# Small first loads of q and k, first weights between two parts, and values used as loaded, in a fused attention and MLP kernel

## The chip, the cores and the metric

The kernel runs on one core of a Trainium2 chip. Times are device microseconds (us) of one execution; "span" is the profiled time from the first to the last instruction. The kernel before takes 306.58 us, the median of three runs (306.48 to 307.78). A difference counts as faster or slower from 2% on.

## The reference

Windowed attention (8 batches, 8 heads, 576 tokens, head size 64; each query sees keys at most 32 positions away), followed by an MLP over all 4608 tokens. Cut to what matters:

```python
scores = (1 / 8) * np.matmul(q, k.transpose(0, 1, 3, 2))
mask = np.abs(pos[:, None] - pos[None, :]) <= 32
attn = softmax(np.where(mask, scores, -1e9))          # without its rows' maximum in the kernel
x = np.matmul(attn, v)                                # -> (4608, 512)
h = x @ w_in                                          # (512, 2048)
out = (h * sigmoid(1.702 * h)) @ w_out                # (2048, 512)
```

## The kernel before

Tokens are worked on in units of 128. A unit is: transpose its keys and queries on TensorE, copy them out of PSUM (keys on VectorE, queries on ScalarE), scores, exp on ScalarE, multiply by a band mask on VectorE, multiply with the values, normalize on VectorE, transpose to xT. Two units make a tile, on which layer 1 (`h_ps`, then gelu) and layer 2 (`o_ps`) work. The program order is written by hand, and each engine runs its own queue in that order. Only the head, up to the first full layer-1 work, is touched by the change:

```python
# head(), order of issue; GpSimd's loads and VectorE's work are recorded in this order
self.load_first("k", 0); self.load_first("q", 0)     # heads 0,1 of 512 tokens, f32, on SyncE
self.setup()                                         # memsets, identity
for h in ((2, 4), (4, 8)):                           # the other heads, cast on the way
    for c in "kq": self.load_heads(0, c, h)
self.load_v(0); self.load_v(1); self.load_v(2, 0, 64)
self.setup_mask()                                    # GpSimd alone: memset, 4 selections
for c in "kq": self.load_edge(c)                     # tokens 512..575
self.load_w_in(0)                                    # first quarter of w_in
...
self.keep_busy(15)                                   # fillers: matmuls on zeros
self.pair_heads("k", 0, 0, dve, ...)                 # VectorE: cast of the first keys (kc)
self.pair_heads("q", 0, 0, act, ...)
...
self.values(0, "hh"); self.norm(0)
self.values(1, "ot"); self.norm(1)
self.x_T(0, "a", act)
self.edge_T("k", "a", dve); self.edge_T("q", "a", act)
self.band(2); self.x_T(1, "o", act); self.scores(3)
l1 = self.layer1_start()                             # first two pairs of layer 1, by halves
...
self.layer1(0, 2); self.x_T(2, "t")                  # second pair
self.layer1(0, 3); self.x_T(3, "o")
self.layer1(0, 4)                                    # from here on TensorE is full
```

A unit's odd half needs values that start 64 tokens later than they are loaded. `odd_v` makes them, by two copies a unit.

The softmax here doesn't subtract the row's maximum and nothing guards it: scores larger than these inputs give would overflow.

Of the kernel before, what the change touches and what calls it, by code (L numbers as in the profile page):

```python
# [27 lines left out]
class _Kernel:  # L28
# [7 lines left out]
    def __init__(self, ctx, tc, q, k, v, w_in, w_out, out):  # L36
        self.tc, self.nc = tc, tc.nc
        self.q, self.k, self.v, self.w_in, self.w_out, self.out = q, k, v, w_in, w_out, out
        self.B, self.H, self.S, self.D = q.shape
        self.N = self.B * self.S  # L40
        self.DM = self.H * self.D
        self.DFF = w_in.shape[1]
        self.NK = self.DM // 128
        self.NFF = self.DFF // 128
        self.scale = 1.0 / (self.D ** 0.5)
        self.NU = self.N // 128
        self.NW = self.NU // 2

        def pool(name, bufs, **kw):
            return ctx.enter_context(tc.tile_pool(name=name, bufs=bufs, **kw))  # L50

        self.cst = pool("cst", 1)
        self.work = pool("work", 2)
        self.ps = pool("ps", 1, space=bass.MemoryType.PSUM)
        self.stage, self.paired, self.turn = {}, set(), {}
        self.xT, self.g, self.o_ps = {}, {}, {}
        self.sc, self.p, self.acc, self.x, self.o_sb = {}, {}, {}, {}, []
# [10 lines left out]
    def setup(self):  # L68
        nc, cst = self.nc, self.cst
        self.ident = cst.tile([128, 128], BF16, name="ident")  # L70
        self.mask = cst.tile([128, 4, SQ], BF16, name="mask")
        self.w_in_sb = cst.tile([128, self.NK, self.DFF], BF16, name="w_in_sb")
# [13 lines left out]
        make_identity(nc, self.ident)  # L86
        for i in range(NV):
            nc.vector.memset(self.ve[i][:, :, self.D:], 1.0)  # L88

    def setup_mask(self):  # L90

        pool, m = self.nc.gpsimd, self.mask
        lo, hi = slice(0, 64), slice(64, 128)
        pool.memset(m, 1.0)
        for blks, rows, sign in ((slice(0, 2), lo, 1), (slice(0, 2), hi, -1), (slice(2, 4), lo, -1), (slice(2, 4), hi, 1)):
            ap = m[rows, blks, :].rearrange("p b (j s) -> p b j s", j=JT)
            pool.affine_select(out=ap, in_=ap, compare_op=ALU.is_ge, fill=0.0, base=0,  # L97
                               pattern=[[0, 2], [-sign, JT], [-sign * JT, SQ // JT]], channel_multiplier=sign)
# [28 lines left out]

    def load_heads(self, i, c, heads=None):

        key = (c, i)  # L130
        if key not in self.stage:
            self.stage[key] = self.work.tile([128, self.H, JT * self.D], BF16, name=c + "s", tag=c + "s", bufs=3)
        lo, hi = heads or (0, self.H)
        src = {"q": self.q, "k": self.k}[c]
        for off, b, s, m in self.pieces(512 * i, 512):
            self.nc.gpsimd.dma_start(self.stage[key][off // JT:(off + m) // JT, lo:hi, :],  # L136
                                     src[b, lo:hi, s:s + m, :].rearrange("h (p j) d -> p h (j d)", j=JT))
# [26 lines left out]
    def heads_T(self, c, i, hp, kind):  # L164


        tp = self.bank(kind, [128, JT, 128], BF16, "tp")
        for j in range(JT):
            if (c, i, hp) in self.paired:
                self.nc.tensor.transpose(tp[:, j, :], self.stage[c, i, "c"][:, hp, j], self.ident)  # L170
                continue
            for t in range(2):
                self.nc.tensor.transpose(tp[64 * t:64 * t + 64, j, :],
                                         self.stage[c, i][:, 2 * hp + t, j * self.D:(j + 1) * self.D], self.ident)
        return tp

    def keys_T(self, i, hp, kind="t", eng=None):
        tp = self.heads_T("k", i, hp, kind)
        at = (512 * i) % RING
        self.cast(eng or self.nc.vector, self.kT[:, hp, at:at + 512].rearrange("r (p j) -> r p j", j=JT),  # L180
                  tp.rearrange("r j p -> r p j"))

    def queries_T(self, i, hp, kind="t", eng=None):
        at = (128 * i) % RP
        tp = self.heads_T("q", i, hp, kind)
        self.cast(eng or nc.vector, self.qT[:, JT * hp:JT * hp + JT, at:at + 128], tp)

    def load_first(self, c, hp):

        raw = self.stage[c, "raw", hp] = self.cst.tile([128, 2, JT * self.D], F32, name=f"{c}_raw{hp}")  # L190
        src = {"q": self.q, "k": self.k}[c]
        self.nc.sync.dma_start(raw, src[0, 2 * hp:2 * hp + 2, 0:512, :].rearrange("h (p j) d -> p h (j d)", j=JT))

    def pair_heads(self, c, i, hp, eng, src=None):
# [3 lines left out]
        self.paired.add((c, i, hp))  # L198
        if src is None:
            src = self.stage[c, i][:, 2 * hp:2 * hp + 2, :]  # L200
        self.cast(eng, self.stage[c, i, "c"][:, hp], src.rearrange("p h (j d) -> p j h d", j=JT))
# [14 lines left out]

    def load_edge(self, c):

        self.stage[c, "edge"] = self.work.tile([64, self.H, self.D], BF16, name="edge", tag="edge")
        src = {"q": self.q, "k": self.k}[c]  # L220
        self.nc.gpsimd.dma_start(self.stage[c, "edge"], src[0, :, 512:576, :].rearrange("h s d -> s h d"))  # L221

    def edge_T(self, c, kind, eng):
        nc = self.nc
        src = self.stage[c, "edge"]
        tp = self.bank(kind, [128, 4, 64], BF16, "tp")
        for hp in range(4):
            nc.tensor.transpose(tp[:, hp, :], src[:, 2 * hp:2 * hp + 2, :], self.ident[:64, :64])
        if c == "k":
            self.cast(eng, self.kT[:, :, 512:576], tp)  # L230
        else:
            self.cast(eng, self.qT[:, :, 128:144].rearrange("r (h j) p -> r h j p", j=JT),
                      tp.rearrange("r h (p j) -> r h j p", j=JT))
# [24 lines left out]
    def band(self, u, hps=range(4)):  # L258
        p = self.p[u]
        cross = [(2 * u + i) % 9 == 8 for i in range(2)]  # L260
        a, b = 0 if cross[0] else 1, 2 if cross[1] else 3
        for eo in range(2):
            pv = p[:, eo, 2 * hps[0]:2 * hps[-1] + 2].rearrange("p (h b) s -> p h b s", b=2)
            msk = self.mask[:, a:b + 1:b - a, :].rearrange("p (o b) s -> p o b s", o=1)
            self.nc.vector.tensor_mul(pv, pv, msk.to_broadcast([128, len(hps), 2, SQ]))  # L265
# [54 lines left out]
    def values(self, u, kinds="aa"):  # L320
        nc, D = self.nc, self.D
        p = self.p.pop(u)
        acc = [self.bank(kinds[i], [128, 4, D + 1], F32, f"pv{i}") for i in range(2)]
        for half in range(2):
            for hh in range(4):
                h = 4 * half + hh
                for blk in range(2):
                    vt = (self.ve, self.vo)[blk][u % NV]
                    nc.tensor.matmul(acc[half][blk * 64:blk * 64 + 64, hh, :], p[:, h % 2, h // 2 * 2 + blk, :],  # L329
                                     vt[:, h, :D + 1], start=(hh == 0), stop=(hh == 3))  # L330
# [72 lines left out]
    def layer1_start(self):  # L403
# [3 lines left out]

        def unit(s):
            for d in range(2):
                self.products1(hps[d], 0, d, slice(128 * s, 128 * s + 128), s == 0, s == 1)  # L410
                if s:
                    self.nc.scalar.activation(g[:, 2 * d:2 * d + 2, :], hps[d], AF.Gelu_apprx_sigmoid)

        return unit
# [53 lines left out]
    def head(self):  # L468
# [5 lines left out]
        for h in ((2, 4), (4, 8)):  # L474
            for c in "kq":
                self.load_heads(0, c, h)
        for m in range(2):
            self.load_v(m)
        self.load_v(2, 0, 64)
        self.setup_mask()  # L480
        for c in "kq":
            self.load_edge(c)
        self.load_w_in(0)
# [17 lines left out]
        self.keep_busy(15)  # L501
        self.pair_heads("k", 0, 0, dve, self.stage["k", "raw", 0])
        self.pair_heads("q", 0, 0, act, self.stage["q", "raw", 0])
        for hp in range(2):
            self.keys_T(0, hp, "ht"[hp], dve)
            self.keep_busy(2)
            self.queries_T(0, hp, "ho"[hp], act)
            self.keep_busy(1 if hp else 2)
# [3 lines left out]
        self.keep_busy(5, "o")  # L512
        for hp in (2, 3):
            self.keys_T(0, hp, "ht"[hp % 2], dve)
        self.keep_busy(5, "o")
        for hp in (2, 3):
            self.queries_T(0, hp, "ho"[hp % 2], (act, dve)[hp % 2])
        self.keep_busy(1, "t")
        self.odd_v(0, dve)
        for u in range(2):  # L520
            self.scores(u, (2, 3))
        self.odd_v(1, act)
        self.band(0, (2, 3))
        self.keep_busy(5)
        self.scores(2)
        self.band(1, (2, 3))
# [4 lines left out]
        self.keep_busy(3)  # L531
        self.x_T(0, "a", act)
        self.edge_T("k", "a", dve)
        self.edge_T("q", "a", act)
        self.band(2)
        self.x_T(1, "o", act)
        self.scores(3)
        l1 = self.layer1_start()
        l1(0)
        self.band(3)  # L540
        self.odd_v(2, dve)
        self.odd_v(3, dve)
        l1(1)
# [24 lines left out]
        for hp in range(4):  # L568
            self.keys_T(1, hp, "a", dve)
            self.queries_T(1, hp, "a", act)  # L570
# [35 lines left out]
        for hp in range(4):  # L606
            self.keys_T(2, hp, "t", dve)
            if hp in (0, 1):
                self.pair_tile(2, (hp + 2,))
            self.queries_T(2, hp, "o", act)  # L610
# [22 lines left out]
    def window_4(self):  # L633
# [36 lines left out]
        for hp in range(4):  # L670
            self.queries_T(3, hp, "t", act)
# [116 lines left out]
```

## Time and profile before

| | kernel before |
|---|---|
| median | 306.58 us |
| span of the profiled run | 304.4 us |
| cast of the first keys | 3.71 us |
| second pair of layer 1 starts | 21.17 us |
| group of 96 layer-1 matmuls starts | 23.63 us |

On the page, these two lines tell that TensorE is the bound, and how much of the chain that ended last is not TensorE:

```profile
PE 291.9 (96%) x3395; PEld 203.8 (67%) x3429; DVE 132.5 (44%) x391; ACT 181.2 (60%) x310; POOL 128.6 (42%) x186
...
PE 89%; POOL 4%; DMA 3%; issue 1%; ACT 1%; DVE 0%; POOLq 0%
```

In the second line GpSimd (POOL) with its load issues and the landing of a weight load make up 7%, all of it in the head.

### The profile page before, as it was taken

To read this page: it belongs to the slowest core of one execution; us is meant where nothing else is said; L and a number is where in the kernel's file an instruction comes from. 1 tells how busy PE (TensorE), PEld (TensorE's weight loads), DVE (VectorE), ACT (ScalarE), POOL (GpSimd) and SP (SyncE) were. 2 spreads that over 40 slices of the span, in tenths; PEclk is the share of its full clock that TensorE was granted. 3 is DMA by queue.
4 is the path that set the end of the run, shared out by engine and by line. 5 is a ranking of instruction groups with operands and counts; after the bars stand their busy time and mean duration, and the time that the engine had idled before them with its cause. 6 is when DMAs were issued, how large, how long until landed. Compare 5 with 4: busy or idle time off the path is not lost.

```text
span 304.4 us, 8079 instructions
## 1 busy us (share of the span) xinstructions
PE 291.9 (96%) x3395; PEld 203.8 (67%) x3429; DVE 132.5 (44%) x391; ACT 181.2 (60%) x310; POOL 128.6 (42%) x186
## 2 busy tenths in 40 slices
PE   8789999999999999999999999999999999999992
PEld 5578755957666666666666666666666666666852
DVE  2681288675580807080708070807070708140011
ACT  3676464795866666666666666666666668424410
POOL 8963555696234363436343534343330301130120
PEclk9999999999999999999999999999999999999998
DMA  8999999999999999999999999999969626162112
GB/s 142 154 194 205 200 184 178 194 169 153 161 155 137 134 117 121 177 138 127 148 170 106 133 137 143 141 131 164 123 54 87 58 48 72 38 58 49 35 32 74
DMA packets 130325, 38.35 MB, mean 126 GB/s; under 512 B 111280, under 2 KB 128048, under 8 KB 130288
## 3 DMA queue, kind: packets, MB, share of 16 engines
q0 software_dynamic: 90032, 27.46, 94.8%
q1 hardware_dynamic: 40112, 10.30, 38.8%
q8 instruction: 27, 0.44, 0.7%
q14 instruction: 10, 0.08, 0.1%
q10 hardware_dynamic: 144, 0.07, 0.1%
HBM read 36.96 MB, written 9.44 MB: 152 GB/s over the span
## 4 chain that ended last, share of the span: by engine, by line
PE 89%; POOL 4%; DMA 3%; issue 1%; ACT 1%; DVE 0%; POOLq 0%
PE h_ps L399 40%; PE o_ps L423 40%; DMA w_in_sb<-in_moe_w_in_dram 3%; PE pv L347 3%; PE sc L285 2%; POOL ve L142 2%; PE tp L170 1%; PE o_ps L448 1%; PE sc L251 1%; PE pv L329 1%; POOL ks L136 1%; POOL qs L136 0%; POOL w_in_sb L112 0%; POOL mask L97 0%; POOL edge L221 0%
## 5 line engine op out<-in xcount | busy, mean ns | idle before, releaser
L399 PE MATMUL h_ps<-xT,w_in_sb 128*128 128x256 bf16 (+1 forms) x1168 | 130.6, 271 | 0.5 <-DMA w_in_sb<-in_moe_w_in_dram 0.3
L423 PE MATMUL o_ps<-w_out_sb,g 128*128 128x512 bf16 x526 | 125.3, 379 | 1.8 <-issue 0.2
L399 PEld LDWEIGHTS <-w_in_sb 128*128 128x128 bf16 x1168 | 112.3, 98 | 17.0 <-DMA w_in_sb<-in_moe_w_in_dram 0.9
L393 ACT ACTIVATE g<-h_ps 128x512 bf16<-128x512 f32 x142 | 84.7, 597 | 61.8 <-PE h_ps L399 61.7
L435 POOL DMA_DIRECT2D out_dram<-o_sb x70 | 44.2, 635 | 144.7 <-DVE rec L357 71.6
L423 PEld LDWEIGHTS <-g 128*128 128x128 bf16 x560 | 53.0, 98 | 57.8
L108 DVE COPY o_sb<-o_ps 128x512 f32<-128x512 f32 x34 | 23.4, 690 | 125.9 <-PE o_ps L423 125.9
L142 POOL DMA_DIRECT2D ve<-in_v_dram x41 | 35.5, 873 | 10.0 <-DMA w_out_sb<-in_moe_w_out_dram 2.8
L289 ACT ACTIVATE pp<-sc 128x512 bf16<-128x512 f32 x44 | 22.7, 602 | 24.7 <-PE sc L285 24.7
L149 POOL DMA_DIRECT2D kn<-in_k_dram x27 | 23.5, 876 | 4.5 <-DMA kn<-in_k_dram 1.9
L108 DVE COPY vo<-ve 64x528 bf16<-64x528 bf16 x69 | 22.5, 326 | 2.3 <-DMA ve<-in_v_dram 0.4
L358 DVE TENSOR_TENSOR x<-pv,rec 128x448 bf16<-128x448 f32 (+1 forms) x52 | 22.1, 425 | 1.8
L456 ACT ACT_TABLE_LOAD x13 | 16.7, 1283 | 0.2
L256 ACT ACTIVATE p<-sc 128x512 bf16<-128x512 f32 (+1 forms) x28 | 12.8, 541 | 2.7 <-PE sc L251 2.7
L108 ACT COPY qT<-tp 128x512 bf16<-128x512 bf16 (+1 forms) x16 | 9.1, 570 | 8.9 <-PE tp L170 6.1
L459 ACT ACT_TABLE_LOAD x11 | 14.1, 1283 | 0.2
L136 POOL DMA_DIRECT2D qs<-in_q_dram x17 | 12.1, 724 | 3.9 <-DMA w_out_sb<-in_moe_w_out_dram 1.8
L265 DVE TENSOR_TENSOR p<-p,mask 128x512 bf16<-128x512 bf16 (+1 forms) x28 | 9.8, 381 | 4.7 <-ACT p L256 2.3
L108 DVE COPY kT<-tp 128x512 bf16<-128x512 bf16 (+1 forms) x13 | 8.5, 658 | 5.1 <-PE tp L170 4.3
L347 PEld LDWEIGHTS <-pp 128*64 128x64 bf16 x384 | 7.1, 110 | 5.1 <-issue 5.1
L108 DVE COPY qc<-qs 128x512 bf16<-128x512 bf16 x32 | 9.3, 335 | 2.4 <-DMA qs<-in_q_dram 2.4
L465 PE MATMUL junk<-idle 128*128 128x256 bf16 x41 | 7.9, 333 | 1.5 <-DVE ve L88 1.1
(76 smaller groups left out, 179.2 us busy)
## 6 DMA issues: line engine op xcount, KB each, us to landing
out_dram<-o_sb POOLq DMA_DIRECT2D x70, 128.0 KB, 6.1
ve<-in_v_dram POOLq DMA_DIRECT2D x31, 128.0 KB, 8.5
kn<-in_k_dram POOLq DMA_DIRECT2D x21, 128.0 KB, 9.5
w_in_sb<-in_moe_w_in_dram POOLq DMA_DIRECT2D x4, 512.0 KB, 9.4
w_out_sb<-in_moe_w_out_dram POOLq DMA_DIRECT2D x4, 512.0 KB, 13.3
qs<-in_q_dram POOLq DMA_DIRECT2D x2, 448.0 KB, 13.2
qs<-in_q_dram POOLq DMA_DIRECT2D x3, 256.0 KB, 7.0
qs<-in_q_dram POOLq DMA_DIRECT2D x2, 384.0 KB, 10.5
```

The costliest lines, as they stand in the source:

```text
L108: (eng.copy if eng is self.nc.scalar else eng.tensor_copy)(out, in_)
L136: self.nc.gpsimd.dma_start(self.stage[key][off // JT:(off + m) // JT, lo:hi, :], src[b, lo:hi, s:s + m, :].rearrange("h (p j) d -> p h (j ...
L142: self.nc.gpsimd.dma_start(self.ve[m % NV][at:at + n, :, :self.D], self.v[b, :, s:s + n, :].rearrange("h s d -> s h d"))
L149: self.nc.gpsimd.dma_start(kn[off:off + n], self.k[b, :, s:s + n, :].rearrange("h s d -> s h d"))
L289: nc.scalar.activation(p[:, eo, 2 * g:2 * g + 2], src, AF.Exp, scale=self.scale)
L347: nc.tensor.matmul(out[blk * 64:blk * 64 + 64, n, :], pq, vt[:, h, :D + 1], start=(h in (0, 7)), stop=(h in (6, 7)))
L358: nc.vector.tensor_mul(x[:, hs, :], src[:, :, :D], rec[:, hs, :].to_broadcast([128, hs.stop - hs.start, D]))
L393: self.nc.scalar.activation(self.g[t][:, 2 * d:2 * d + 2, :], hps, AF.Gelu_apprx_sigmoid)
L399: self.nc.tensor.matmul(hps[:, i, cols], self.w_in_sb[:, kr, ff * 128:(ff + 1) * 128], self.xT[t][:, kr, cols], start=(first and i == 0 an ...
L423: nc.tensor.matmul(o_ps, self.g[t][:, ff, s * 128:(s + 1) * 128], self.w_out_sb[:, ff, :], start=(ff == 0), stop=(ff == self.NFF - 1))
L435: self.nc.gpsimd.dma_start(self.out[row + 64 * blk:row + 64 * blk + 64, :].rearrange("(s j) f -> j s f", j=JT), o_sb[64 * blk:64 * blk + 64])
L456: self.nc.scalar.activation(self.spark, self.spark, AF.Gelu_apprx_sigmoid)
```

## The change

Its intent: the first loads are smaller, so the first units can start sooner; the first quarter of w_in comes sooner; the 64 edge tokens, which were loaded twice, are loaded once; and the copies of odd values of the first four units go. Its core (cuts marked):

```diff
+        self.mask_hi = cst.tile([128, 2, SQ], BF16, name="mask_hi")
+        nc.vector.memset(self.mask, 1.0)
+        nc.vector.memset(self.mask_hi[0:64, 1, :], 0.0)
     def setup_mask(self):
-        pool.memset(m, 1.0)
-        # four selections, each over two blocks of the mask
+        # four selections, each over one block of the mask
+        for b in (1, 0):
+            self.nc.vector.tensor_copy(self.mask_hi[64 * b:, b, :], m[64 * b:, 2 * b + 1, :])
+        for b in (0, 2):
+            self.nc.vector.tensor_copy(m[:, b, :], m[:, b + 1, :])
...
+        return {"a": (0, 320), "b": (320, 256), 1: (576, 448)}.get(i) or (512 * i, 512)
...
     def values(self, u, kinds="aa"):
+        # units 0..3: odd half = upper rows of ve[u] and, in 4 more matmuls a half, lower rows of ve[u + 1]
...
     def head(self):
-        for h in ((2, 4), (4, 8)):
-            for c in "kq":
-                self.load_heads(0, c, h)
+        for c in "kq":
+            self.load_heads("a", c, (2, 4))
+        make_identity(nc, self.ident)
+        for c in "kq":
+            self.load_heads("a", c, (4, 8))
         (v 0, 1 and half of 2)
+        self.load_w_in(0)
         self.setup_mask()
         for c in "kq":
-            self.load_edge(c)
-        self.load_w_in(0)
+            self.load_heads("b", c)
...
-        self.keep_busy(15)
+        self.keep_busy(13)
...
+        self.keep_busy(9)
         self.x_T(0, "a", act)
-        self.edge_T("k", "a", dve)
-        self.edge_T("q", "a", act)
-        self.band(2)
-        self.x_T(1, "o", act)
-        self.scores(3)
-        ... layer1_start by halves, band(3), odd_v(2), odd_v(3) in between
+        self.keep_busy(5)
+        self.x_T(1, "a", act)
+        gelu = self.layer1_start()
+        # keys_T("b"), queries_T("b") for two pairs of heads each, 3 to 8 fillers after each
+        for u in (2, 3):
+            self.scores(u)
+            self.band(u)
+        gelu()
+        self.keep_busy(6, "o")
```

## The prediction

> **What bounds the kernel now.** I read the page first: TensorE is busy 96% of a span of 304.4 us. Next the chain that ended last, in order of time; then the timeline of its first 24 us; last, busy time by stretch. In the chain (start, length, what) the bound changes hands once:
>
> ```profile
> 13.44 0.70 POOL w_in_sb L112
> 14.14 9.45 DMA w_in_sb<-in_moe_w_in_dram
> 23.59 0.05 issue
> 23.63 10.65 PE h_ps L399 x96
> ```
>
> Up to 23.6 us the chain is GpSimd issuing loads and a weight load landing. From 23.63 us (the layer-1 group that needs the third quarter of w_in) it is TensorE's own work. The stretches from 25 to 280 us have TensorE idle for only 2.0 us of 255. So I treat all after 23.63 us as a fixed 280.7 us of work, and ask at what time the changed kernel reaches that same group.
>
> The timeline gives the durations for the head (start, length, engine, line, operation, in brackets the idle time before and its releaser):
>
> ```profile
> 1.14 3.38 PE L465 MATMUL junk<-idle 128*128 128x256 bf16 x15 [1.14 <-DVE ve L88]
> 3.71 0.48 DVE L108 CAST kc<-k_raw 128x512 bf16<-128x512 f32 x1 [2.42 <-DMA k_raw<-in_k_dram]
> ...
> 4.63 2.50 POOL L142 DMA_DIRECT2D ve<-in_v_dram  x3
> ...
> 7.52 1.56 POOL L97 TENSOR_SCALAR_AFFINE_SELECT mask<-mask 64x128 bf16<-64x128 bf16 x4
> ...
> 8.06 1.21 ACT L256 ACTIVATE p<-sc 128x256 bf16<-128x256 f32 x4 [0.35 <-PE sc L251]
> 8.08 0.72 PE L465 MATMUL junk<-idle 128*128 128x256 bf16 x5
> ...
> 9.12 0.90 DVE L265 TENSOR_TENSOR p<-p,mask 128x256 bf16<-128x256 bf16 x4 [1.97 <-POOL mask L97]
> ...
> 18.27 1.28 ACT L412 ACT_TABLE_LOAD   x1
> ...
> 21.17 1.05 PE L399 MATMUL h_ps<-xT,w_in_sb 128*128 128x256 bf16 x8 [0.33 <-DMA w_in_sb<-in_moe_w_in_dram]
> ```
>
> To be seen: VectorE casts the first keys at 3.71 us, as soon as they land, long before the mask exists (9.08 us). Only its first mask multiplication waits for the mask, 1.97 us. Exp of units 2 and 3, gelu and values lie close behind one another, and layer 1 starts its second pair at 21.17 us.
>
> **What the Trainium skill says.** "TensorE: Matmul & The Clock Gate", section on the HAM clock gate, Part 1: VectorE's and ScalarE's queues are strict FIFO, TensorE alone pulls weight loads ahead; so an instruction behind a waiting one waits too. The trace before agrees, in that no engine runs its instructions out of the program's order. The same Part 1: the array's clock is halved after an idle window of about 3.4 us and restored after a busy one. The trace agrees: the first 15 fillers take 3.38 us (225 ns each), while later five take 0.72 us (about 110 ns each when the roughly 0.2 us of pipeline at the end is taken off). "ScalarE: Activation LUTs", section "What ACT_TABLE_LOAD costs": about 1283 ns; the trace has 1.28 us.
>
> **The change part by part.** Three things are meant to help. The first loads carry 320 instead of 512 tokens. The first quarter of w_in is issued at about 7.15 us, not at 10.4. The odd-value copies of units 0 to 3 (eight pieces on VectorE and ScalarE, 0.3 to 0.6 us each) are gone, for 8 small matmuls and four extra multiplications a unit. But the order of instructions in the two built programs shows a fourth: the mask is now finished by four copies on VectorE, which wait for GpSimd's last mask selection, and they stand ahead of the cast of the first keys. In the kernel before nothing stands there.
>
> Step 1, when the mask is done. GpSimd starts at 0.82 us: loads of k and q 0.86 + 0.76, identity 0.55, gaps 0.15, loads of k and q 0.77 + 0.74, three of v 2.45, w_in 0.77: about 7.95 us. Four selections of half the size: between half and all of the 1.56 us, I take 1.25: 9.2 us. Four small copies, an estimate of 0.5 us from the 0.21 us of a 128x256 copy: 9.7 us. The cast (0.48) ends at 10.2 us, where it ended at 4.19. This is 6.0 us on the path.
>
> Step 2, to the first exp. Before, from the cast's end to exp 3.87 us, some 0.7 of it for loads which will now have landed. But TensorE, out of fillers at about 4.1 us, stands idle for 6 us and begins at half clock: transposes of 0.63 instead of 0.39 us, fillers of 0.21 instead of 0.11. TensorE's run of 24 transposes and 8 fillers takes about 3.8 us. I take 4.5: exp at 14.7 us, 6.6 late.
>
> Step 3, to x of units 0 and 1. Eight multiplications by the two masks at 0.385 us a pair, but the key copy for the other four heads stands behind four pairs: 16.65, and 0.86 us for 640 columns (0.69 for 512): 17.5. Query copy 17.85, scores 0.3, exp from 18.15, first unit masked at 19.3, second at 20.05. Values in fillers' shadow; two norms of 1.15 us, all on VectorE: 22.3. Second transpose of x: 22.6 us (16.0 to 16.5 before).
>
> Step 4, to the queries of the second part. The started layer 1 takes 2.0 us as before (1.96): 24.6. Its weights landed at about 13.5 us by my count: gain of 3.5 us that nothing uses. Now the second part's keys and queries, landed at about 15 and 16.5, are transposed: four groups at 0.4 us, and 14 fillers between at 0.11: 27.7; last query copy 0.6: 28.3 us. Before, the 64 edge tokens took this place with 8 transposes, already done at 16.1.
>
> Step 5, to the steady state. Scores 0.65, four exps 2.2, table load 1.28, first gelu 0.6: 33.05 us. Only then is the PSUM bank free for the second pair of layer 1 (21.17 before). The pair 0.9, transpose 0.25, the next pair 0.85, transpose 0.25: the group that started at 23.63 starts at about 35.3 us.
>
> Sum: 35.3 - 23.63 = 11.7 us. Of it 6 to 6.6 are steps 1 and 2; the other 5 are the second part standing in a row behind the first layer 1, where the kernel before overlapped units 2 and 3 with units 0 and 1. Later there is nothing to win back but a little of the 2.0 us of idle time, as loads will be far ahead: -0.3. One batch less of 64 tokens and two fewer load issues are hidden. 306.58 + 11.4 = 318.0 us.
>
> **The rivals.** First, the weights' landing stays the bound. For it: the 9.45 us DMA link of the chain. The bytes ahead of the third quarter of w_in are nearly the same (320 + 256 tokens against 512 + 64), so it lands at about 23.4 us by my count, and if TensorE were ready by then the time would be 306 to 307. Against it: exp of unit 3, the table and gelu cannot come before the second part's queries, landing at 16.5; even without any stall this chain reaches the second pair at 22.3 or later against 21.17. So there is hardly a way to be faster.
>
> Second, the mask stall is hidden, since the first multiplication waited for the mask anyway until 9.08. Then only the serial second part counts: all from step 3 on about 5.8 us earlier, group at 29.5, time about 312.2. Against it: behind the mask come not only multiplications but also casts and copies that feed TensorE; scores can't start before them.
>
> Third, the half clock lasts: idle stretches longer than the fillers cover keep the array cold through the whole head of some 20 us of small matmuls. It would add 2 to 4 us: 320 to 322. Against it: there are 76 fillers, 41 before.
>
> **Range and chances.** My steps are sums of measured durations, but semaphore waits, the cold stretch and the size of selections can each be off by 0.5 to 1 us, in either direction; the second and third rivals bound it. 8 in 10: 314.5 to 321.5. Slower by over 2% means above 312.7: 0.94. Within 2%: 0.05. Faster by over 2%: 0.01.
>
> **What would show it.** The cast of the first keys at 9.5 to 10 us, with VectorE's wait for GpSimd's mask in front, some 6 to 7 us long; TensorE idle from about 4 to 10 us; first exp at 14 to 15.5; the first layer-1 matmuls at about 22.5, with w_in not the releaser; second pair at about 33; no weight landing in the last chain, but the mask, VectorE and ScalarE. From the first full-width o_ps group on, the two timelines should differ by a constant. I am wrong if the cast still starts near 3.5 us, if the h_ps group of 96 starts before 30 us, or if the steady part's length changes by over 1 us.

## The result, and the profile after

The changed kernel takes 321.0 us (median of four runs, 319.15 to 322.42), beside 307.11 us of the kernel before (306.48 to 307.78) in the same rounds. The ratio is 1.0448, with a 95% interval of 1.0388 to 1.0509. Ratios here are the mean time of one kernel's fast runs over that of the other's of the same rounds, so not quite the ratio of the medians. It is slower. The profiled run is the fastest of the four, 319.15 us with a span of 317.4.

The two lines of its page that answer to those of before:

```profile
PE 301.3 (95%) x3518; PEld 210.2 (66%) x3552; DVE 133.0 (42%) x402; ACT 180.4 (57%) x309; POOL 127.6 (40%) x183
...
PE 93%; POOL 2%; DVE 1%; issue 1%; ACT 1%; POOLq 0%
```

The landing of weights has left the chain altogether, as the change wished, and yet the span is 13.0 us longer. TensorE's share of the chain rose, but not by useful work: fillers and half-speed matmuls count too. The chain in order of time (start, length, what):

```profile
9.30 0.40 DVE mask_hi L102
9.74 0.28 DVE kc L114
10.06 0.45 PE tp L183 x4
...
23.81 1.85 PE h_ps L420 x32
...
34.52 0.98 PE h_ps L420 x8
...
36.81 10.48 PE h_ps L420 x96
```

The group of 96 starts at 36.81 us, not 23.63: 13.18 us later, which is the whole difference of the spans (13.0). The timeline of the head shows how it comes to that:

```profile
7.86 1.22 POOL L99 TENSOR_SCALAR_AFFINE_SELECT mask<-mask 64x64 bf16<-64x64 bf16 x4
...
9.11 0.59 DVE L102 COPY mask_hi<-mask 64x64 bf16<-64x64 bf16 x2 [7.52 <-POOL mask L99]
...
9.56 0.45 DVE L114 CAST kc<-k_raw 80x512 bf16<-80x512 f32 x1
...
10.06 0.45 PE L183 MATMUL tp<-ident,kc 80*128 80x80 bf16 x4 [5.97 <-DVE kc L114]
...
13.93 1.21 ACT L255 ACTIVATE p<-sc 128x256 bf16<-128x256 f32 x4 [0.47 <-PE sc L250]
...
15.39 0.74 POOL L118 DMA_DIRECT2D w_in_sb<-in_moe_w_in_dram  x1 [1.22 <-DMA w_in_sb<-in_moe_w_in_dram]
...
30.02 2.06 ACT L255 ACTIVATE p<-sc 128x512 bf16<-128x512 f32 x4 [0.41 <-PE sc L250]
...
34.45 1.05 PE L420 MATMUL h_ps<-xT,w_in_sb 128*128 128x256 bf16 x8
```

VectorE waits 7.52 us for the mask in front of a cast whose data had long landed; TensorE then waits 5.97 us for the cast. The issue at 15.39 us is the fourth quarter of w_in. It waited for a load of w_in to land, in the order of issue the first: so the first quarter landed at about 15.3 us, and layer 1 used it only at 23.72.

The other three runs are 1.9 to 3.3 us slower than the profiled one, and their mean granted clock is lower: 0.992, 0.992 and 0.984 against 0.998. The experiments show what that is.

### The profile page after: what moved, and what is told of

Read it like the earlier page. It is cut to its first block, busy times and chain, and to the rows that moved or that the text cites. A ratio compares the mean times of both kernels' runs of the same rounds, so it can differ in the third digit from the quotient of the medians.

```text
span 317.4 us, 8333 instructions
## 1 busy us (share of the span) xinstructions
PE 301.3 (95%) x3518; PEld 210.2 (66%) x3552; DVE 133.0 (42%) x402; ACT 180.4 (57%) x309; POOL 127.6 (40%) x183
## 4 chain that ended last, share of the span: by engine, by line
PE 93%; POOL 2%; DVE 1%; issue 1%; ACT 1%; POOLq 0%
PE h_ps L420 39%; PE o_ps L445 38%; PE junk L487 3%; PE pv L368 3%; PE sc L301 2%; PE pv L349 2%; PE tp L183 2%; PE sc L250 1%; PE tp L186 1%; PE o_ps L470 1%; POOL ve L152 1%; PE tp L405 1%; DVE p L281 1%; POOL qs L146 0%; ACT g L414 0%
## 5 line engine op out<-in xcount | busy, mean ns | idle before, releaser
L159 POOL DMA_DIRECT2D kn<-in_k_dram x27 | 23.6, 878 | 7.1 <-DMA kn<-in_k_dram 3.3
L379 DVE TENSOR_TENSOR x<-pv,rec 128x448 bf16<-128x448 f32 (+1 forms) x52 | 22.1, 425 | 1.8
L114 DVE COPY vo<-ve 64x528 bf16<-64x528 bf16 x63 | 19.7, 313 | 1.8
L114 ACT COPY qT<-tp 128x512 bf16<-128x512 bf16 (+3 forms) x16 | 8.9, 556 | 16.6 <-PE tp L183 12.0
L114 DVE COPY kT<-tp 128x512 bf16<-128x512 bf16 (+3 forms) x12 | 7.8, 646 | 20.2 <-PE tp L183 15.7
L487 PE MATMUL junk<-idle 128*128 128x256 bf16 x76 | 14.7, 337 | 1.1 <-DVE idle L84 1.1
L487 PEld LDWEIGHTS <-idle 128*128 128x128 bf16 x76 | 7.4, 115 | 3.3 <-DVE idle L84 1.1
L114 DVE COPY qc<-qs 128x512 bf16<-128x512 bf16 (+1 forms) x32 | 9.6, 343 | 0.0
```

The source lines that it names most:

```text
L114: (eng.copy if eng is self.nc.scalar else eng.tensor_copy)(out, in_)
L159: self.nc.gpsimd.dma_start(kn[off:off + n], self.k[b, :, s:s + n, :].rearrange("h s d -> s h d"))
L379: nc.vector.tensor_mul(x[:, hs, :], src[:, :, :D], rec[:, hs, :].to_broadcast([128, hs.stop - hs.start, D]))
L487: self.nc.tensor.matmul(junk, self.idle[:, 0:128], self.idle, start=True, stop=True)
```

## The experiments

Theory: two parts of the head cost about 13 us between them, the mask copies in front of the cast (with the half clock that the idle stretch brings), and the second part standing in a row behind layer 1. Rivals: the stall is hidden; the half clock or the fillers (matmuls on zeros) do it; the early weights are worth something. All twelve kernels, with the start of the group of 96 in the profiled run:

| run | group of 96 | median us (range) | ratio |
|---|---|---|---|
| before | 23.63 | 307.11 (306.48 to 307.78) | 1 |
| after | 36.81 | 321.00 (319.15 to 322.42) | 1.0448 |
| e1_copies_late (wrong result) | 41.48 | 324.41 (323.02 to 327.50) | 1.0589 |
| e2_warm | 36.17 | 318.31 (317.09 to 319.03) | 1.0377 |
| e3_stall_in_before | 28.46 | 310.63 (310.50 to 312.51) | 1.0140 |
| e4_no_fillers | 37.53 | 318.32 (317.79 to 324.81) | 1.0371 |
| e5_copies_late2 | 36.65 | 318.86 (315.90 to 319.29) | 1.0359 |
| e6_fill_exps | 37.68 | 320.09 (319.82 to 320.57) | 1.0429 |
| e7_second_part_first | 30.48 | 315.06 (312.31 to 317.36) | 1.0233 |
| e8_values_in_before | 24.91 | 308.73 (307.26 to 312.21) | 1.0047 |
| e9_late_warm | 31.38 | 314.34 (313.85 to 317.10) | 1.0263 |
| e10_first_warm | 31.23 | 313.50 (312.56 to 313.72) | 1.0216 |
| e11_weights_after | 36.57 | 319.10 (318.58 to 322.31) | 1.0429 |
| e12_reordered | 28.68 | 311.38 (310.93 to 312.17) | 1.0157 |

Each call of four had its own runs of the kernel before: 306.46, 306.62 and 306.21 us. Medians and ranges are of all runs; the ratios leave out the slowest runs of e4 (324.81), e7 (317.36) and e8 (312.21), which count as slow, being over 1.5% above the fastest of their kernel.

**e3_stall_in_before: the stall alone, in the kernel before.**

```diff
         self.setup_mask()
+        seen = self.cst.tile([128, 1], BF16, name="seen")
+        dve.tensor_copy(seen, self.mask[:, 3, 0:1])
```

> The kernel before with one added instruction: a VectorE copy of one mask column ahead of the cast of the first keys, so that the cast waits for GpSimd's last mask selection (about 9.1 us) as in the changed kernel. Theory (the stall alone makes a good third of the loss): cast at about 9.3 instead of 3.71 us; some of the 5.6 us overlaps waits that were there anyway (loads 0.5 + 0.9, mask 1.97), so the group of 96 goes from 23.63 to about 27.6 us and the time from 307 to about 311. Rival (hidden): 307 to 308. Rival (full length, plus a cold array): 313 or more.

```profile
9.11 0.16 DVE L482 COPY seen<-mask 128x1 bf16<-128x1 bf16 x1 [7.83 <-POOL mask L97]
9.18 0.42 DVE L108 CAST kc<-k_raw 128x512 bf16<-128x512 f32 x1
```

The cast starts at 9.18 us, as VectorE waited 7.83 us for the mask, and the group of 96 starts at 28.46. One copy of a single column, in the wrong place of a queue, costs 4.83 us of the group's start and 310.63 us against 306.46. Of the cast's 5.47 us of delay only 0.6 was hidden. In time this is 1.4%, but the interval of the ratio (1.0109 to 1.0172) leaves out 1. The theory's size (4) was a little low; "hidden" and "full length and more" fall.

**e2_warm: fillers through the stall.**

```diff
-        self.keep_busy(13)
+        self.keep_busy(58)
```

> The changed kernel with 58 fillers at the start instead of 13, so that TensorE is busy until about 9.5 us, through VectorE's wait. Theory (the array was at half clock after 6 us of idleness, and this is some 1 us of the loss): 32 scores take about 0.45 us instead of 0.64 and two fillers 0.38 instead of 0.63 right after the stall, first exp about 0.6 us earlier than 13.93, the group of 96 about 1.0 us earlier than 36.81, time about 319 to 320. Rival (the half clock is hidden behind VectorE and ScalarE): the small matmuls get shorter, but the group starts within 0.3 us of 36.81.

First exp 12.66 instead of 13.93 us, and the second pair of layer 1 starts at 32.14 instead of 34.45. So the cold array cost 2.3 us by then, more than twice what I expected. But the group starts only 0.64 us earlier, because in this execution something else came in between. The view of busy time by stretch of e2 gives from and to, length, busy time and instructions of PE, weight loads, DVE, ACT and POOL, then the granted clock, the share of DMA and GB/s:

```profile
29.00:32.40 3.40, 2.66 (x51) 2.10 (x52) 3.19 (x13) 3.15 (x5) 0.88 (x1) 1.00 1.34 200
32.40:35.90 3.50, 3.50 (x23) 2.61 (x21) 1.23 (x4) 0.60 (x1) 1.36 (x2) 0.51 1.42 200
```

From 32.4 to 35.9 us the array ran at half speed, right after a stretch in which TensorE waited for exp and masks of units 2 and 3. Eight matmuls of 256 columns took 1.63 us there instead of 1.05. A spell of 3.4 us at half clock costs 1.7 us. The same spell is in e4 (33.9 to 37.3 us, 0.51). The profiled run of the changed kernel has none, and its mean clock is 0.998 (the cold start does not count in that mean: full clock is on record from 19.1 us, in the kernel before from 5.1). And 3.4 us at half clock lower the mean over 317 us by 0.005, so its runs at 0.992 fit one spell, and that at 0.984 two or three; no trace of them was kept, so this is an inference. e11, which has the same head but for one order, gives the relation once more: its runs at 0.998 to 0.999 take 318.58 to 319.32 us, that at 0.992 takes 321.04, that at 0.984 takes 322.31. The relation doesn't hold everywhere: e4's two runs at 0.976 take 318.25 and 318.32 us, as little as its two at 0.997 (317.79 and 318.21).

**e6_fill_exps: fillers where that spell begins.**

```diff
-        self.keep_busy(6, "o")
+        self.keep_busy(16, "o")
         self.values(2)
         self.norm(2)
+        self.keep_busy(5, "o")
         self.values(3)
```

> The changed kernel with 16 fillers instead of 6 after the scores of units 2 and 3 and 5 more between their values. In the runs so far a stretch of 3.4 us at half clock falls at about 32.4 to 35.9 us in some executions and not in others (mean granted clock 0.992 to 0.993 with one, 0.998 without). Theory (TensorE is too idle while it waits for exp and masks of units 2 and 3, so that the clock falls back, at 1.7 us each): with fillers nearly all executions have clock 0.997 or more and take 319 to 319.8, group of 96 at about 37.0. Rival (the spell has nothing to do with idleness): spread of 319 to 322.5 and clocks down to 0.984 as before.

All six runs lie within 0.75 us (319.82 to 320.57), where the changed kernel's four lay within 3.27. The group starts 0.87 us later (37.68), but 0.54 of this lies ahead of the added fillers: the first layer 1 ends at 26.13 instead of 25.59 us, as full clock is on record from 20.2 instead of 19.1 us in this execution. So the fillers cost about 0.3. The median is 0.9 lower than the changed kernel's, which is within the noise (intervals of the ratios 1.0400 to 1.0458 and 1.0388 to 1.0509). The spread agrees with the theory; my words on the clock do not: two of the six runs have a mean clock of 0.973 and 0.978 and are no slower than the rest, so the mean alone doesn't tell where a spell fell. And one trace speaks against the theory as I put it. In the changed kernel's profiled run TensorE counts as busy for only 2.46 of the 3.41 us from 29.33 to 32.74, and the clock stays full; in e2 it is busy for 2.71 of the 3.41 us ahead of its spell (29.04 to 32.45). So too little busy time alone doesn't bring the spell, and why it comes in some executions and not in others stays open.

**e4_no_fillers: the 17 fillers between layer 1 and the scores of unit 2.**

```diff
             self.keys_T("b", [n, n + 1], "ot"[n // 2], (dve, act)[n // 2])
-            self.keep_busy(3)
-        self.keep_busy(5)
...
             self.queries_T("b", [n, n + 1], "ot"[n // 2], (dve, act)[n // 2])
-            self.keep_busy(3)
```

> The changed kernel without the 17 fillers between the first layer 1 and the scores of units 2 and 3. Theory (this part is TensorE's own row, so fillers there are on the path): four groups of transposes take 1.5 us, but two of them wait for a PSUM bank to be emptied, so scores of unit 2 start about 1.2 us after where fillers would let them less: 28.2 instead of 29.35 us, and the group of 96 at about 35.6 instead of 36.81; time about 319.5. Rival (the fillers stand in the shadow of the copies): group within 0.3 us of 36.81. Rival (without them the clock falls back): later than 36.81.

From the end of the first layer 1 to the scores it is now 2.1 us (26.2 to 28.31) instead of 3.8 (25.6 to 29.35): the fillers were on the path, with 1.65 us. The group was late all the same, at 37.53: full clock came 1.1 us later than in the changed kernel (20.2 against 19.1 us in the trace's record of the clock; this is ahead of the edit and the same in e6, so a matter of the execution), and then the spell took 1.7. The theory holds; the clock did fall back, as the rival says, but as e2 keeps these fillers and has the spell too, their removal is not shown to be the cause. The median, 318.32, is 2.7 us under the changed kernel's. These 17 are not all: of the first 40 us of the changed kernel's chain 24.0%, 9.6 us, are fillers. What the others cost, and how much of them only fills waits, no run tested.

**e1_copies_late: a failed experiment.**

```diff
-        (the four mask copies in setup_mask)
+        self.mask_copies()          # the same four, in front of the first scores
```

> The changed kernel with its four mask copies moved on VectorE behind the second key copy, in front of the first mask multiplication; nothing else differs. Theory (the stall is on the path): the cast of the first keys goes from 9.56 us to about 3.5, but the first multiplication still has to wait for the mask until about 9.75, so not all of the 6 us come back: about 4.5 us, the layer-1 group of 96 starts at about 32.3 us instead of 36.81, and the time falls from about 320 to 315.5. Rival (the stall is hidden, as the mask is needed then anyway): under 1 us comes back, 319 to 320. Rival (the stall costs its full length): 6 us or more, 314 or less.

The result is wrong (relative error 0.21), and it wasn't meant to be. Moving the copies put them behind the memsets that cut the mask at the batches' ends, so they waited for these and then overwrote them:

```profile
16.76 0.40 DVE L107 COPY mask<-mask 128x64 bf16<-128x64 bf16 x2 [6.98 <-POOL mask L113]
```

The cast had gone to 3.45 us as wished, but VectorE stood still from about 9.8 to 16.76 us. It tests nothing that was asked; it shows a second time what a waiting copy at the head of a queue does.

**e5_copies_late2: the same, mended.** GpSimd makes the whole mask again; VectorE's two copies into the second mask stand behind the second key copy.

```diff
+        for blks, rows, sign in (...):                # as in the kernel before
-        (four copies ahead of the first cast)
+    def mask_copies(self):                            # called ahead of the first scores
+        for b in (1, 0):
+            self.nc.vector.tensor_copy(self.mask_hi[64 * b:, b, :], self.mask[64 * b:, 2 * b + 1, :])
```

> Mends the first try, whose mask copies came behind the later memsets of the mask and so waited for them too. Here GpSimd makes the mask alone, as in the kernel before (four selections over two blocks, 1.56 us), and VectorE only copies two blocks into the second mask, behind the second key copy. Theory (stall on the path): cast at about 3.5 us instead of 9.56; the first multiplication starts at about 9.9 when the mask is there; scores of the other four heads at about 12.6 instead of 17.64; group of 96 at about 31.6 instead of 36.81; time 314 to 316 (the upper end if the array falls back to half clock once). Rival (hidden): 319 or more.

Up to the scores of heads 4 to 7 everything came as expected, 12.65 us instead of 17.64. Then all of it was lost again, and the group starts at 36.65. A line of the timeline of e5, and then its busy time by stretch, show where:

```profile
12.65 0.65 PE L250 MATMUL sc<-qT,kT 64*64 64x64 bf16 x32 [3.48 <-DVE kT L114]
```

The columns of the stretches are as in e2:

```profile
9.00:12.70 3.70, 0.22 (x6) 0.05 (x8) 2.88 (x11) 0.36 (x1) 3.63 (x7) 0.88 1.36 158
12.70:22.00 9.30, 9.30 (x112) 6.92 (x113) 4.20 (x16) 1.80 (x5) 6.99 (x13) 0.50 1.51 187
```

Without the stall TensorE runs early through its work and then waits 3.48 us for the mask (through the key copy behind the multiplications). The clock falls at 11.8 us, and the array crawls until 22.1, then once more from 32.3 to 35.7. By its time alone this run would have spoken for the rival "hidden"; its clock says that it tested something else as well.

**e9_late_warm: e5 with TensorE kept busy.**

```diff
         self.queries_T("a", [2, 3], "h", act)
-        self.keep_busy(4, "o")
+        self.keep_busy(34, "o")
...
-        self.keep_busy(6, "o")
+        self.keep_busy(13, "o")
         self.values(2); self.norm(2)
+        self.keep_busy(3, "o")
```

> The mended kernel with late copies, and TensorE kept busy in the two stretches in which its clock fell there: 34 fillers instead of 4 while the mask is awaited (TensorE idled from 9.2 to 12.65 us and ran at half clock from 11.8 to 22.1), and 13 + 3 instead of 6 during the exps. Theory (the stall costs about 5 us, but its removal only moved the idle stretch, and the half clock ate the gain): scores of heads 4 to 7 stay at about 12.7 us, no half clock after 5 us, group of 96 at about 32 us instead of 36.65, time about 314.5. Rival (the 5 us were never there to be had): group above 35 us, time above 317.5.

The same stretches as above, now of e9:

```profile
9.00:12.70 3.70, 3.54 (x33) 2.93 (x30) 2.88 (x11) 0.46 (x1) 3.63 (x7) 1.00 1.31 145
12.70:22.00 9.30, 9.30 (x185) 7.96 (x186) 4.52 (x17) 2.97 (x7) 7.05 (x13) 1.00 1.45 176
```

The clock stays at full, and the group starts at 31.38 us, 5.43 earlier than in the changed kernel; the time is 314.34 us. So the copies in front of the cast cost about 5.4 us with the cold array they cause, in good accord with the 4.83 of e3. The rival falls.

**e7_second_part_first and e10_first_warm: the second part ahead of layer 1.** e7 is e5, with

```diff
         self.x_T(0, "a", act)
+        self.keys_T("b", [0, 1], "o", dve)
         self.x_T(1, "a", act)
+        self.keys_T("b", [2, 3], "t", act)
+        (queries of the second part)
-        gelu = self.layer1_start()
-        (keys and queries of the second part)
         (scores and masks of units 2 and 3)
+        gelu = self.layer1_start()
         gelu()
```

> The mended kernel of this call (copies late) with keys, queries, scores, exp and masks of the second part put before the first layer 1 instead of after it; the rest as there. Theory (standing in a row behind layer 1 is the other part of the loss): the queries of the second part land at about 18.7 us, scores of unit 2 at about 20.5, layer 1 runs in the shadow of exp, first gelu at about 24.6, group of 96 at about 27.5 us, 4 us earlier than in the kernel with late copies; time about 310. It isn't below 307, as the third quarter of w_in lands at about 25 us. Rival (the row costs little, the queries' landing is what counts): within 1.5 us of the kernel with late copies.

e10 is e7 with the 34 fillers of e9 while the mask is awaited.

> The kernel with the second part first, with 34 fillers instead of 4 in the same stretch. Theory: the half-clock spell of 12.4 to 15.8 us goes, x of units 0 and 1 about 1 us earlier, group of 96 at about 29.3 us instead of 30.48, time 310.5 to 312. Compared with late copies kept warm this puts the row behind layer 1 at some 2.5 to 3 us. Rival: nothing gained (the second part's queries, landing at 18.7 us, set the time): group at 30.2 or later.

e7 reaches the group at 30.48 us, with one cold spell, from 12.4 to 15.8. Against e5 (36.65) that is 6.2 us, but e5 lost several us to its own spells, so the comparison flatters. The fair one is e10 against e9, as both are kept warm up to 22 us. There the second pair of layer 1 begins at 26.37 us instead of 29.02, 2.65 earlier, which is what I had expected of this row. Not all of it is the order: e7 and e10 also have 12 fillers between the transpose of the first x and the scores of unit 2, where e5 and e9 have 22, and in the two chains these take 1.72 and 2.82 us. On the other hand e10 comes to the scores of heads 4 to 7 0.47 us later than e9 (13.17 and 12.70). With both taken off, and 0.1 for e9's fillers in the exps, the order alone is worth about 1.9 us by my estimate, the length of the first layer 1 (1.85) that now lies beside the exps. Then e10's clock falls:

```profile
27.20:30.60 3.40, 3.14 (x17) 2.38 (x18) 0.69 (x2) 0.60 (x1) 0.88 (x1) 0.50 1.24 206
```

It stops 0.81 us in its pair, runs 3.4 us at half speed, and reaches the group at 31.23, only 0.15 before e9. My expectation for the group (29.3) was missed. In times e10 is 0.8 us better than e9 (313.50 and 314.34). The row behind layer 1, with its fillers, is thus worth some 2.65 us at the second pair, and in the profiled execution a spell took most of it back. e7's runs spread over 5 us; in the profiled one an xT transpose by DMA at 101 us landed late besides, and TensorE waited 1.3 us for it.

**e8_values_in_before: values as loaded, alone, in the kernel before.**

```diff
-        self.odd_v(0, dve) ... self.odd_v(3, dve)
+        (mask_hi, its two copies ahead of the first scores, band_first and values() as in the change)
```

> The kernel before with only the third part of the change: units 0 to 3 take the values as loaded (masks of two kinds, 8 more small matmuls a unit, no odd-value copies), the two mask copies behind the second key copy. Theory (this part is nearly neutral): 12 more multiplications of 0.22 to 0.28 us on VectorE against six odd-value copies of 0.3 to 0.4 saved there and two of 0.63 on ScalarE; group of 96 between 23.5 and 24.5 us, time 306.3 to 307.5. Rival (it costs over 1 us, as VectorE's multiplications delay the key copies of heads 4 to 7): 308 or more.

I expected this to be neutral. It isn't: the group starts at 24.91 us, 1.28 later, and the time is 308.73 us against 306.62 (ratio 1.0047, interval 1.0013 to 1.0081). The rival named the size (308 or more). The profiled run also takes 1.1 us more after the group than the kernel before (281.9 and 280.7 us), which is not explained. Two things show in the head. VectorE's first four multiplications took 0.90 us; two mask copies and eight multiplications now take 2.2, so the key copies for heads 4 to 7 begin at 11.31 instead of 9.93 us. And in the chain of that run the values of two units stand with

```profile
14.79 1.96 PE pv L357 x48
```

for 48 matmuls, 0.041 us each from start to start, where the 16 of a unit in the kernel before all begin within 0.28 us (13.56 to 13.84), 0.018 us apart. In the timeline a group of four half-height matmuls takes as long as one of eight full ones, about 0.245 us.

**e11_weights_after: the first weights behind the second part.**

```diff
-        self.load_w_in(0)
+        self.load_heads("b", "k")
         self.setup_mask()
-        for c in "kq":
-            self.load_heads("b", c)
+        self.load_heads("b", "q")
+        self.load_w_in(0)
```

> The changed kernel with one order of issue turned round: second part's keys, mask, second part's queries, and only then the first quarter of w_in (so the weights aren't between the two parts any more). Theory (the early weights gain nothing, for layer 1 starts at 23.7 us and its weights landed at about 15): weights land at about 18.5 us, nothing waits for them, group of 96 within 0.4 us of 36.81, time 319 to 322.5 as the changed kernel. Rival (the early weights are worth something): more than 1 us later.

The weights are issued at 9.63 us instead of 7.08, nothing waits for them, and the group starts at 36.57 us, 0.24 earlier. The median is 319.1 us. The early weights are worth nothing here.

**e12_reordered: an attempt to save the plan.** It joins e7's order and e11's order of issue, puts key copies, queries and scores of heads 4 to 7 ahead of all mask multiplications, and fills the waits.

```diff
         for u in range(2):
             self.scores(u, (0, 1))
-            self.band(u, (0, 1))
         (keys, queries of heads 4 to 7)
         for u in range(2):
             self.scores(u, (2, 3))
+        self.mask_copies()
+        for u in range(2):
+            self.band(u, (0, 1))
+            self.band(u, (2, 3))
```

> An attempt to save the plan of small first loads: late copies; key copies, queries and scores of heads 4 to 7 ahead of the mask multiplications; the second part loaded ahead of the first weights and used before layer 1; fillers in the waits. Theory (what then bounds the head is the landing of the third quarter of w_in, about 24.9 us, 1.3 us later than in the kernel before, as the small first loads leave the DMA rings short of work at 4 to 6 us: 97 GB/s against 136): group of 96 at 25 to 26.5 us, time 308 to 310, still not below the kernel before. Rival (it beats the kernel before): below 306.3.

311.38 us, the best of the variants of the change, with all six runs at a clock of 0.998 or more. It is still 1.57% slower than the kernel before (the interval, 1.0130 to 1.0185, leaves out 1), and my expectation for it was missed by 2.2 us in the group (28.68 against at most 26.5).

```profile
20.24 0.50 PE sc L250 x24
...
21.42 0.59 ACT p L255
...
24.89 1.01 PE pv L349 x22
```

These are lines of its chain. Not the landing of weights bounds it, but the chain of scores, exp, masks and values of units 2 and 3, which starts at 20.24 us there; in the kernel before unit 2 has its scores at 13.2 and unit 3 at 16.5. No run gave a version that beats the kernel before.

## Why the prediction was right

The time lies in the range, and the group's start, which carried the estimate, was forecast at 35.3 us and measured at 36.81. The median of 321.0 is 3 us above the 318.0 named and 0.5 below the range's end, and one of the four runs (322.42) lies outside; the profiled run (319.15) is 1.15 above. Step by step:

- **Step 1, the mask copies ahead of the cast.** Right, with its cause: selections from 7.86 us (7.95 was taken, though the addends named sum to 7.87), 1.22 us long (1.25), cast ending at 10.01 (10.2). e3 and e9 put the whole stall, cold array included, at 4.8 to 5.4 us; "6 to 6.6" counted nothing as hidden, and was 1 us too much.
- **Step 2, the cold array.** The mechanism is right, but the size was taken in the wrong place. The first exp came at 13.93 (14.7), but the loss went on until full clock at 19.1 us, and e2 shows 2.3 us by the second pair. Step 3 had taken fillers and values at full speed.
- **Step 3, to x of units 0 and 1.** Key copy, exp and masks fell within 0.5 us of the forecast. "Values in fillers' shadow" was wrong: they are in the chain with 1.95 us, nine fillers behind them with 1.09 and five more with 0.55. VectorE was done with x at 22.62 us (22.3 forecast). The second transpose of x came at 23.6 us by the chain (22.6). This is 1.0 of the missing 1.5 us.
- **Step 4, the weights and the second part.** "Gain of 3.5 us that nothing uses" is right that nothing uses it (e11). The landing was mis-sized: about 15.3 us, not 13.5. The small first loads seem to leave the DMA rings short of work (no run tests this alone); between 4 and 6 us they move 97 GB/s where the kernel before moved 136. The line of that stretch of the kernel before, with GB/s as its last number:

```profile
4.00:6.00 2.00, 1.77 (x17) 1.13 (x15) 0.88 (x2) 1.03 (x2) 2.00 (x3) 1.00 1.15 136
```

and of the changed kernel:

```profile
4.00:6.00 2.00, 0.09 (x1) 0.00 (x0) 0.00 (x0) 0.62 (x1) 2.00 (x4) 1.00 0.82 97
```

From the end of layer 1 to the scores I had 3.7 us, and 3.76 was measured.
- **Step 5, to the steady state.** Scores to second pair: 5.1 us (4.75 forecast); from there to the group 2.36 (2.25). These 0.46 us are the rest of the missing 1.5. But the size came out by another path, and that is luck. The forecast summed exps, table load and first gelu, and had no mask multiplications. In the chain the second pair follows the values of units 2 and 3, and these wait for eight multiplications on VectorE, from 30.65 to 33.35 us:

```profile
30.04 0.59 ACT p L255
...
32.93 0.43 DVE p L281
33.35 0.10 DVE rec L389
...
33.50 1.02 PE pv L349 x22
34.52 0.98 PE h_ps L420 x8
```

The first of the two gelus, which begin at 33.40 and take 1.09 us together, was over some 0.5 us before the pair began. Eight multiplications instead of four are part of using the values as loaded: in the kernel before, those of units 2 and 3 take 0.75 and 0.91 us.
- **The sum's second term** ("the other 5 are the second part standing in a row") was right in sum and too simple in cause. The row is worth 2.65 us at the second pair (e10 against e9), of which 1.1 are fillers. The values as loaded, which I had counted as a help, cost 1.28 us (e8). Stall, row and values together (5.4, 2.65 and 1.28) make 9.3 of the 13.2 us. e12, which mends stall and row, is still 5.05 us late, and what of this is the values' part, what the fillers and what the later arrival of the second part wasn't separated by a run. It stays open.
- **The third rival** was partly true. I had it as a half clock through the whole head. In fact there is the cold start, up to 19.1 us, and after it spells of 3.4 us (10.2 once, in e5), and the one that falls in the exps of units 2 and 3 is the likely reason why the median (321.0) lies 1.85 us above the profiled run, near the upper end of the range. This rests on the traces of e2, e4, e5 and e10, the mean clocks of the other runs, and the narrow spread of e6; the changed kernel's own slower runs have no trace, so it is not shown.

## What to carry to other kernels

Before moving a small piece of work to another engine, look at what stands behind it in that engine's queue: a copy of 0.16 us (e3) that waits for a slow engine costs what follows it nearly the whole wait (4.83 of 5.47 us), and the order of instructions shows it before any run. A head of small matmuls must be judged with the clock beside it, for a gain that lets TensorE idle elsewhere can be eaten by half-speed spells (e5), and two kernels can be compared fairly only when both are warm (e9) and have the same fillers (e10). And an operand that arrives sooner is worth nothing until the chain that uses it is the one that waits for it.

## What the Trainium skill lacked or had wrong

- "TensorE: Matmul & The Clock Gate", HAM clock gate, Part 1: it speaks of an idle window of about 3.4 us. Here the window need not be idle throughout: in e5 the clock fell at 11.81 us, 2.6 us after the last matmul before a wait, and in the 3.41 us up to then TensorE still counts as busy for 0.77. The clock also fell after a stretch without any long gap: in e2 from 29.04 to 32.45 us TensorE counts as busy for 2.71 of 3.41 us, with waits of 0.5 us at most, and the clock was half from there on. The page's section on a second failure mode tells of micro-idling between groups, which may be the same; it gives no share of busy time at which this begins. The runs give none either: in the changed kernel's profiled run 2.46 of 3.41 us (29.33 to 32.74) were enough to keep full clock.
- "DMA: Bandwidth & Descriptors", the anatomy of a load issued by GpSimd, calls the making of descriptors small. In the first 16 us of the traces before and after, each such issue holds GpSimd for 0.65 to 0.93 us almost whatever its size (0.65 to 0.75 us for the first loads of 80 partitions, 0.76 to 0.86 for those of 128). That smaller first loads therefore left the rings at 97 instead of 136 GB/s fits this, and no run tests it alone.
- No page has it: matmuls that alternate between full and half height (128 and 64 rows of the array) came at 0.041 us each from start to start (48 in 1.96 us, e8), where those of full height alone came at 0.018 (16 in 0.28 us, kernel before). Whether it is the change of height or the order of accumulation was not tested.
